# Second parity's keys and queries by seven block products, its values beside FFN chunks 0 and 1

## The chip, the cores and the metric

The kernel runs as one launch on one core of a Trainium2 chip. The metric is the device time of that launch in microseconds (us); smaller is better. A core has a matrix engine (PE in the profile, with PEld for its weight loads), two elementwise engines (DVE and ACT), a slower one that here only issues accumulating transfers (POOL), and SP, which issues most of the transfers. Each engine works through its own list of instructions, and instructions wait on semaphores for other engines and for transfers.

## What is computed

Input x has 2048 tokens of 512 channels. Two branches are mixed by a gate per token:

```python
g = sigmoid((x * gate_w).sum(-1, keepdims=True))
q, k, v = split(x @ wqkv)          # 32 heads of 16
# each token attends to itself and 7 earlier tokens at distance 2, 4, ... 14
a = softmax(q . k_window / 4) . v_window @ wo
b = (gelu(x @ w_gate) * (x @ w_up)) @ w_down     # 1792 hidden columns
out = g * a + (1 - g) * b
```

All of it is fp32.

## The kernel before, in words

**Tokens.** A token attends only to tokens of its own parity (the distance is even), so the program works through the even tokens and then through the odd ones: `par` 0 and 1. A parity has 8 tiles of 128 tokens (`jj`), in two blocks of four (`blk`). The 512 input channels are four chunks `kc` of 128.

**Products.** An fp32 operand is split into a high part (a copy to fp32r, "hi") and the rest ("lo", a subtraction); a product is three matmuls, hi.hi, lo.hi and hi.lo. So a tile of 128 tokens by 512 columns over two chunks is 6 matmuls, and a block product (four tiles) 24.

**Seven products.** Where a product is a 2 by 2 of blocks (two token blocks, two halves of the channels, two halves of the columns), `start()` for the keys and queries of the first parity and `gate_up()` for each FFN chunk form seven block products in place of eight: a11.b11, a12.b21, s1.t1, s2.t2, s3.t3, s4.b22 and a22.t4, where s1 to s4 are sums of blocks of x and t1 to t4 sums of blocks of the weights. The second parity's keys and queries are not formed so: `project(1, 0)` (L221) makes those of the first 16 heads (column block `cb` 0) tile by tile with 12 matmuls of 512 columns, and `project_one` (L251) those of the other 16 heads (`cb` 2), again 12 for each tile. `qkv_mm` (L183) issues them.

**Order of the program.** `start()` (from L842) loads x and the weights of the first parity, makes its keys and queries and prepares FFN chunk 0. `ffn(0)` runs 14 FFN chunks (`gate_up` and, two chunks behind, `down`); the first parity's values (`values`) run between its first products. Then comes what I call the turn: `project(1, 0)`, the split of more weights, `project(1, 1)` (the values), then `ffn(1)`, whose chunks 0 and 1 have the tiles of `project_one` between their products. In the last chunk (13) of `ffn(0)` the steps of `before()` and, after it, of `again` and `split_kq` prepare the turn: x of the second parity is split on DVE (copy and subtraction), and the weights of the first 16 heads, which `early()` loads in chunk 12, by ACT and DVE. The sums of x for the FFN are made by `sums_x()` within `project(1, 0)`.

**Attention.** It runs on DVE as a generator of small steps, pulled by credit (`pull`) as the matmuls are written: per unit of 8 heads (`par`, `u`) four pairs of score products (L290, L293), a softmax, and four pairs of weighted sums (L331 to L339). A unit's keys and queries go through HBM (`KS`, `QS`) and are loaded shifted (`load_kq`), the values likewise (`VS`, L274 and L275), and so are the outputs (`OS`, L346), which the output projection at the end reads (`finish`).

**What sets the order.** The scheduler of the language places instructions on their engines by its own estimate of time; `high_priority` puts attention behind the matmul chain, `paced` ties an instruction to the last matmul written, and the helper `Row` (`row`, `act`, `mms`) keeps the DVE, ACT and PE instructions written through it in the order written. Buffers are rings by tag: `raw` (2), `S` (8), `g0` and `g1` (2 each), `d` (4), `s` (3), `c` (4), `r` (2), PSUM banks `p` (4) and `acc0` to `acc3`. A tile of a ring waits until the tile that had its place has been read.

**Lines that the steps touch.** L107 loads x of the second parity into `raw`; L532 copies a running sum from SBUF to a PSUM bank before a `down`, L554 back; L549 scales the last `down` of parity 0 into an `s` tile and L550 sends it to the output by POOL; L452 and L453 (ACT, then a POOL transfer that accumulates) form the lo part of FFN weights, L457 the hi part; L464 and L470 store FFN weight sums and parts for the second parity; L590 and L606 are the two GELUs of a chunk, and L606's first after an exponential loads its table.

Of the kernel before, what the change touches and what calls it, by code (L numbers as in the profile page):

```python
# [16 lines left out]
P = 128  # L17
# [16 lines left out]
FILLERS = 2  # L34
BEHIND = 150
PACE = (0.9, 1.0, 1.12)
LOAD = 4.0
BT = 4
# [9 lines left out]
def tile_gated_mix(ctx: ExitStack, tc: tile.TileContext, xt, wqkv, wff, wo, out):  # L48
# [66 lines left out]
    def split_x(par, blk, kc, cols=((0, 512),), copy=None, eng=nc.vector):  # L115
        if blk and kc < 2:
            X[par, blk, kc] = tl("rt", F32R), tl("rt", F32R)
        hi, lo = X[par, blk, kc]
        raw = XR[kc % 2][:, (2 * blk + kc // 2) * 512:]
        for a, n in cols:  # L120
            c = slice(a, a + n)
            split(eng, hi[:, c], lo[:, c], raw[:, c], copy)

    def sums_x():

        for n in ("s1", "s2", "s4", "s3"):
            for kc in range(2):
                XOP[n, kc] = pair("S")
        for kc in range(2):
            a11, a12, a21, a22 = (XR[kc][:, i * 512:(i + 1) * 512] for i in range(4))  # L130
            nc.vector.tensor_tensor(a22, a21, a22, op=OP.add)
            nc.vector.tensor_tensor(a21, a11, a21, op=OP.subtract)
            nc.vector.tensor_tensor(a11, a22, a11, op=OP.subtract)
            nc.vector.tensor_tensor(a12, a12, a11, op=OP.subtract)
            for n, x in ("s1", a22), ("s2", a11), ("s4", a12), ("s3", a21):
                split(nc.vector, *XOP[n, kc], x)
                yield

    def rooms():

        def of(*tags):
            for tag, n in tags:
                t = tl(tag, F32R)
                w = 512 if n == 4 else WA
                yield from (t[:, i * w:(i + 1) * w] for i in range(n))
        cols = of(("g1", 4))
        for _ in range(2):
            yield next(cols), next(cols)
        for _ in range(2):
            yield pair("S")  # L150
        cols = of(("g0", 3), ("g1", 3), ("c", 1), ("c", 1))
        for _ in range(KC):
            yield next(cols), next(cols)
        for _ in range(KC):
            yield pair("d")

    def load_kq_weights(raw, kc):
        nc.sync.dma_start(raw[:, :512], wqkv[0, kc // 2, :, kc % 2 * 512:kc % 2 * 512 + 512])

    def held(o, i):  # L160
        return paced(nc.scalar.activation(o, i, AF.Copy))

    def load_cb(cb, kc, tag, room, late=False):
        hi, lo = WC[cb, kc] = next(room)
        raw = tl(tag)
        n = 512
        if cb == 1:
            nc.sync.dma_start(raw[:, :CU], wqkv[1, 2, :, kc * WQ:kc * WQ + CU])
            nc.sync.dma_start(raw[:, CU:CU + WQ], wqkv[0, 2, :, kc * WQ:(kc + 1) * WQ])
            n = CU + WQ  # L170
        else:

            queue = nc.scalar if cb == 0 and kc < 2 else nc.sync
            queue.dma_start(raw[:, :n], wqkv[cb // 2, kc // 2, :, kc % 2 * 512:kc % 2 * 512 + 512])
        return lambda: split(nc.vector, hi[:, :n], lo[:, :n], raw[:, :n], held if late else None)
# [4 lines left out]
    names = iter(["acc0", "acc1", "acc2", "acc3", *["p"] * 4])  # L180
# [27 lines left out]
    def take(ps, par, jj, hh, vals, tag=None):  # L208
        st = tl(tag or next(stages))[:, :512]
        n = CU if vals else 512  # L210
        nc.scalar.activation(st[:, :n], ps[:, :n], AF.Copy)
        two = st.rearrange("p (a c d) -> p a c d", a=2, c=2)
        dst = VS[par, hh] if vals else KS[par, hh]
        queue = nc.sync if (vals if par else not vals) or hh and not vals else nc.scalar
        queue.dma_start(rows(dst[:, W:], jj), two[:, 0])
        if not vals:
            queue.dma_start(rows(QS[par, hh], jj), two[:, 1])
        elif not hh:
            nc.scalar.activation(z[:, par, jj:jj + 1], ps[:, CU:CU + 1], AF.Copy)

    def project(par, cb, bg=iter(())):  # L221
        for jj in range(NP):
            if cb == 1:
                for hh in range(2):

                    ps = bank(f"acc{(2 * jj + hh) % BT}")
                    qkv_mm(ps, par, jj, 1, range(KC), (CU, 0)[hh], (WQ, CU)[hh])
                    take(ps, par, jj, hh, True)
            else:
                ps = bank(next(names))  # L230
                qkv_mm(ps, par, jj, 0, range(KC))
                take(ps, par, jj, 0, False)
            next(bg, None)
            pull((2.7, 2.2)[par])
        done.add((par, cb))
    def gates(par, ex):
        ordered(nc.scalar.activation(en, z[:, par], AF.Exp, scale=-1.0), ex)
# [4 lines left out]
    def values(jj):  # L242
        for hh in range(2):
            ps = bank(f"acc{(2 * jj + hh) % BT}")
            qkv_mm(ps, 0, jj, 1, range(KC), (CU, 0)[hh], (WQ, CU)[hh])
            take(ps, 0, jj, hh, True, tag=None if jj < 5 else "c")
        pull(2.7)
        if jj == NP - 1:
            done.add((0, 1))

    def project_one(par, jj):  # L251

        ps = bank(f"acc{jj % BT}")
        qkv_mm(ps, par, jj, 2, range(KC))
        take(ps, par, jj, 1, False, tag=None if jj < 5 else "c")
        pull(2.2)
        if jj == NP - 1:
            done.add((par, 2))

# [41 lines left out]
    def softmax(par, u):  # L301
# [7 lines left out]
        if not u:  # L309
# [4 lines left out]
        nc.vector.reciprocal(m, m)  # L314
        nc.vector.tensor_tensor(m, m, g[:, par, None, :].to_broadcast([P, UH, NP]), op=OP.mult)
# [51 lines left out]
    def attention():  # L367
# [8 lines left out]
        for i, un in enumerate(units):  # L376
            if scored == i:
# [5 lines left out]
                mixed = False  # L383
            yield from softmax(*un)

# [224 lines left out]
    SPLIT = []  # L610

    def again(blk, kc):

        split_x(1, blk, kc, copy=lambda *x: paced(nc.vector.tensor_copy(*x)))
# [9 lines left out]
    def split_kq():  # L624
        kc, raw = SPLIT.pop(0)
        hi, lo = WC[0, kc] = next(room)
        split(nc.vector, hi, lo, raw, held)

    def before():

        room_x(1)
        yield
        again(0, 0)
        yield
        again(0, 2)
        yield
        split_kq()
        SPLIT.append((3, tl("r")))
        load_kq_weights(SPLIT[-1][1], 3)
        yield  # L640
        split_kq()

    def ffn(par):
# [3 lines left out]
        for f in range(FC):  # L647
# [38 lines left out]
            else:  # L686
# [8 lines left out]
                if f + 2 == FC:  # L695
                    at(8, early)
# [474 lines left out]
```

## Time and profile before

| | |
|---|---|
| median of 3 runs | 605.52 us (605.47 to 606.92) |
| the profiled execution | 605.68 us, of which 603.9 us are the span of instructions |
| PE busy | 597.0 us, 99% of the span, 2802 matmuls |
| DVE busy | 525.1 us, 87% |
| ACT busy | 383.4 us, 63% |
| granted TensorE clock | 0.999 |
| HBM read, written | 67.18 MB, 36.77 MB |

The profile gives, for each engine, the time in which instructions ran. Matmuls are pipelined, so the length of one in the profile (390 ns for 512 columns) is not the distance between two; that is read from the starts of a run of them. The views used are: the page's totals, the list of waits (who waited for whom), the timeline of one engine (start, length, instruction, idle time before it and what ended it), busy time by stretch, and the transfers by line with their time from issue to landing.

### The profile page before, as it was taken

To read this page: it belongs to the slowest core of one execution; us is meant where nothing else is said; L and a number is where in the kernel's file an instruction comes from. 1 tells how busy PE (TensorE), PEld (TensorE's weight loads), DVE (VectorE), ACT (ScalarE), POOL (GpSimd) and SP (SyncE) were. 2 spreads that over 40 slices of the span, in tenths; PEclk is the share of its full clock that TensorE was granted. 3 is DMA by queue.
4 is the path that set the end of the run, shared out by engine and by line. 5 is a ranking of instruction groups with operands and counts; after the bars stand their busy time and mean duration, and the time that the engine had idled before them with its cause. 6 is when DMAs were issued, how large, how long until landed. Compare 5 with 4: busy or idle time off the path is not lost.

```text
span 603.9 us, 8190 instructions
## 1 busy us (share of the span) xinstructions
PE 597.0 (99%) x2802; PEld 497.9 (82%) x2802; DVE 525.1 (87%) x611; ACT 383.4 (63%) x650; POOL 79.0 (13%) x106
## 2 busy tenths in 40 slices
PE   9999999999999999999999999999999999999997
PEld 6889977788888888878899888888888888888885
DVE  5998869999898999898989978879899999998941
ACT  6845557787678767875553356565866676677531
POOL 0501001111111111102000001111111111101200
PEclk9999999999999999999999999999999999999999
DMA  7289886999889898967889968786887768837823
GB/s 282 84 257 243 244 268 175 277 240 255 238 246 259 222 271 213 263 197 205 261 253 292 299 191 242 169 249 179 209 221 202 210 174 228 245 90 204 115 63 139
DMA packets 84741, 131.03 MB, mean 217 GB/s; under 512 B 8030, under 2 KB 52317, under 8 KB 84700
## 3 DMA queue, kind: packets, MB, share of 16 engines
q1 hardware_dynamic: 63310, 94.01, 48.2%
q0 software_dynamic: 12096, 31.40, 27.6%
q10 hardware_dynamic: 9294, 5.11, 2.8%
q8 instruction: 22, 0.36, 0.3%
q14 instruction: 19, 0.16, 0.1%
HBM read 67.18 MB, written 36.77 MB: 172 GB/s over the span
## 4 chain that ended last, share of the span: by engine, by line
PE 87%; DMA 5%; DVE 3%; ACT 3%; issue 1%; SPq 1%; DVEq 0%; ACTq 0%
PE p L495 40%; PE p L538 12%; PE acc L538 12%; PE acc L189 9%; PE p L767 5%; PE p L834 3%; PE acc L834 3%; PE p L189 2%; PE acc L767 2%; DMA kq<-qs 1%; DMA raw<-wff 1%; DVE prod L290 1%; DMA ws<-g 1%; DMA raw<-xt 1%; DMA ks<-hl 0%
## 5 line engine op out<-in xcount | busy, mean ns | idle before, releaser
L495 PE MATMUL p<-S,g 128*128 128x512 f32 x672 | 166.5, 390 | 0.1
L495 PEld LDWEIGHTS p<-S,g 128*128 128x128 f32 x672 | 125.7, 188 | 26.6 <-ACT rt L554 0.5
L495 PE MATMUL p<-A,g 128*128 128x512 f32 x504 | 127.6, 390 | 0.0
L495 PEld LDWEIGHTS p<-A,g 128*128 128x128 f32 x504 | 94.3, 188 | 19.9 <-DVE c L505 0.3
L290 DVE TENSOR_TENSOR prod<-kq 128x2048 f32<-128x2048 f32 x32 | 73.0, 2282 | 10.1 <-DMA kq<-qs 5.1
L453 POOL DMA_DIRECT2D g<-raw x40 | 34.6, 866 | 334.8 <-ACT g L452 208.1
L331 DVE TENSOR_TENSOR prod<-v,lg 128x2048 f32<-128x2048 f32 x32 | 72.9, 2277 | 5.3 <-PE acc L538 2.5
L293 DVE TENSOR_REDUCE lg<-prod 128x128 f32<-128x2048 f32 x32 | 73.0, 2283 | 0.3
L538 PE MATMUL p<-d,hh 128*128 128x512 f32 x224 | 68.1, 390 | 1.0 <-ACT hh L511 0.5
L538 PE MATMUL acc<-d,hh 128*128 128x512 f32 x224 | 62.1, 391 | 0.5 <-DVE d L87 0.5
L538 PEld LDWEIGHTS p<-d,hh 128*128 128x128 f32 x224 | 41.8, 188 | 10.5 <-ACT hh L511 0.9
L538 PEld LDWEIGHTS acc<-d,hh 128*128 128x128 f32 x224 | 41.9, 188 | 10.2 <-DVE d L87 0.9
L457 ACT ACTIVATE g<-raw 128x1024 fp32r<-128x1024 f32 (+1 forms) x40 | 39.5, 990 | 13.2 <-PE p L495 13.2
L452 ACT ACTIVATE g<-raw 128x1024 fp32r<-128x1024 f32 (+1 forms) x40 | 39.4, 985 | 5.9 <-DVE raw L434 4.8
L505 DVE TENSOR_TENSOR c<-p,s 128x512 f32<-128x512 f32 x56 | 37.9, 681 | 5.6 <-PE p L495 5.6
L509 DVE TENSOR_TENSOR c<-c 128x512 f32<-128x512 f32 x56 | 38.2, 683 | 4.9 <-ACT c L606 4.8
L538 PE MATMUL p<-d,hl 128*128 128x512 f32 x112 | 42.3, 389 | 0.0
L500 ACT ACTIVATE s<-p 128x512 f32<-128x512 f32 x56 | 33.2, 592 | 13.6 <-PE p L495 11.8
L512 DVE TENSOR_TENSOR hl<-c,hh 128x512 fp32r<-128x512 f32 x56 | 38.2, 684 | 2.7 <-ACT hh L511 2.5
L511 ACT ACTIVATE hh<-c 128x512 fp32r<-128x512 f32 x56 | 35.1, 626 | 8.4 <-DVE c L509 7.7
L335 DVE TENSOR_TENSOR prod<-prod 128x1024 f32<-128x1024 f32 x32 | 39.0, 1220 | 0.4
L554 ACT ACTIVATE rt<-p 128x512 f32<-128x512 f32 x48 | 28.1, 593 | 16.2 <-PE p L538 15.9
(193 smaller groups left out, 915.7 us busy)
## 6 DMA issues: line engine op xcount, KB each, us to landing
g<-raw POOLq DMA_DIRECT2D x27, 512.0 KB, 6.5
raw<-wff SPq DMA_DIRECT2D x42, 256.0 KB, 3.2
ws<-g SPq DMA_DIRECT2D x14, 768.0 KB, 5.6
g<-ws SPq DMA_DIRECT2D x14, 768.0 KB, 6.1
r<-wff SPq DMA_DIRECT2D x28, 256.0 KB, 3.9
d<-r POOLq DMA_DIRECT2D x26, 256.0 KB, 6.6
g<-raw POOLq DMA_DIRECT2D x13, 384.0 KB, 6.3
v<-vs SPq DMA_DIRECT2D x8, 512.0 KB, 7.6
```

The costliest lines, as they stand in the source:

```text
L189: LAST[:] = [nc.tensor.matmul(ps[:, :cn], a[:, t], w[:, c0:c0 + cn], start=(kc == 0 and n == 0), stop=(kc == KC - 1 and n == 2))]
L290: paced(nc.vector.tensor_tensor(prod, spans(k, jj), q[:, jj:jj + 2, None, :].to_broadcast([P, 2, W, UC]), op=OP.mult))
L293: nc.vector.tensor_reduce(two_of(lg, jj), prod.rearrange("p j w (h d) -> p (j w) h d", d=DH), axis=AX.X, op=OP.add)
L331: paced(nc.vector.tensor_tensor(prod.rearrange("p j w (h d) -> p (j w) h d", d=DH), spans(v, jj).rearrange("p j w (h d) -> p j w h d", d=D ...
L335: nc.vector.tensor_tensor(prod[:, :, :4], prod[:, :, :4], prod[:, :, 4:], op=OP.add)
L452: nc.scalar.activation(lo, raw, AF.Copy, scale=-1.0)
L457: ins = nc.scalar.activation(hi, raw, AF.Copy)
L495: LAST[:] = [nc.tensor.matmul(ps, w_, a_, start=(start and kc == 0 and n == 0), stop=(kc == 1 and n == 2), skip_group_check=True)]
L509: nc.vector.tensor_tensor(ge, ge, up, op=OP.mult)
L512: nc.vector.tensor_tensor(hl_, ge, hh_.bitcast(F32), op=OP.subtract)
L538: ins = nc.tensor.matmul(pp, a[:, ts], w, start=(i == 0 and n == 0 and gr == 0), stop=(i == 1 and n == 2), skip_group_check=True)
L767: ins = nc.tensor.matmul(pa, a, b, start=(first and n == 0), stop=(last and n == 2), skip_group_check=True)
```

## The change

1. The first parity's weight sums t1 to t4, split into parts, are stored to HBM when they have been made (1 MB each, `store`), so that the second parity can load them (`load`).
2. `project`, `project_one`, `sums_x`, `again`, `split_kq`, `early`, `load_cb` and `rooms` go. In chunk 13 of `ffn(0)` and beside its last downs, `before()` and `ready()` load the raw blocks b11, b21 and b22 of the weights, split a11, a12, b11 and b21 (hi on ACT, lo on DVE) and make and split s1.
3. `kq_second()` makes the second parity's keys and queries by seven block products, in the order a11.b11, a12.b21, s2.t2, s3.t3, a22.t4 (after which the first 16 heads are complete), s1.t1, s4.b22. Attention steps are pulled after each tile (`ASK`).
4. The second parity's values move into chunks 0 and 1 of `ffn(1)`, in the place of `project_one`; the down weights of chunks 0 and 1 are split as in the first parity.
5. The first unit of the second parity does its softmax without the gate, then the scores of the second unit, and only then waits for the values (`gated`).

```diff
-    def early():
-        t = tl("g0")
-        for kc in range(3):
-            raw = t[:, kc * 512:(kc + 1) * 512]
-            load_kq_weights(raw, kc)
-            SPLIT.append((kc, raw))
...
     def before():
         room_x(1)
+        for k in range(2):
+            for i, (n, blk, kc) in enumerate((("a11", 0, 0), ("a12", 0, 2))):
+                OP_[n, k], SRC[n, k] = X[1, blk, kc + k], XR[k][:, i * 512:(i + 1) * 512]
+        load_raw("b11", slots("g1", 4), 0, 0)
         yield
-        again(0, 0)
-        yield
-        again(0, 2)
-        yield
-        split_kq()
-        SPLIT.append((3, tl("r")))
-        load_kq_weights(SPLIT[-1][1], 3)
-        yield
-        split_kq()
+        for step in (("a11", 0), (), (), ("a11", 1), ("a12", 0)):
+            if step:
+                hi(*step)
+                lo(*step)
+            yield
...
+    def load_raw(n, rooms_, hh, half):
+        raw = tl("S")
+        nc.sync.dma_start(raw, wqkv[hh, half, :, :1024])
+        name(n, pairs(rooms_), halves(raw))
+    def store(n, i, t, m):
+        nc.sync.dma_start(TS[n][i:i + m].rearrange("i p c -> p i c"), tiled(t, m))
+    def load(n, i, t, m):
+        nc.sync.dma_start(tiled(t, m), TS[n][i:i + m].rearrange("i p c -> p i c"))
...
+    def ready():
+        q = Q2["q"] = [[XR[k][:, i * 512:(i + 1) * 512] for i in range(4)] for k in range(2)]
+        load_raw("b21", slots("g0", 3, WA) + slots("c", 1), 0, 1)
+        load_pairs("t2")
+        yield
+        for steps in (("b11", 0),), (("b11", 1),), (("a12", 1), ("b21", 0)), (("b21", 1),):
+            for step in steps:
+                hi(*step)
+                lo(*step)
+            yield
+        load_raw("b22", [None] * 4, 1, 1)
...
+    def kq_second():
+        load("t4", 0, t, 4)
+        for i, tag in enumerate("sssc"):
+            t = tl(tag, F32R)
+            load("t3", i, t, 1)
+        U = [bank(f"acc{t}") for t in range(BT)]
+        block(U, "a11", "b11", True, ask=ASK)
+        V_ = [bank("p") for _ in range(BT)]
+        for t in range(BT):
+            out_of(V_[t], U[t])
+        block(V_, "a12", "b21", False, ask=ASK)
...
+        block(U, "s2", "t2", False, ask=ASK)
+        block(U, "s3", "t3", False, ask=ASK)
+        block(U, "a22", "t4", False, ask=ASK)
+        done.add((1, 0))
+        block(Z_, "s1", "t1", True, ask=ASK)
+        for t in range(BT):
+            join(1, BT + t, Z_[t], u3[t])
+        block(Z_, "s4", "b22", False, ask=ASK)
+        for t in range(BT):
+            join(1, t, Z_[t], u2[t])
+        done.add((1, 2))
...
-    room = rooms()
     keep(0)
     ffn(0)
-    for kc in range(KC):
-        load_cb(1, kc, "c", room)()
-    project(1, 0, sums_x())
-    for kc in range(KC):
-        load_cb(2, kc, "r", room, True)()
-    fetch_d(0)
-    for f in range(2):
-        fetch_sums(f)
-    project(1, 1, chain(*(operands(1, 0, i) for i in range(2))))
+    kq_second()
     ffn(1)
```

More of the change, by code (lines that the diff above doesn't have):

```diff
@@ L34 @@
 FILLERS = 2
+ASK = 1.0
 BEHIND = 150
@@ L113, in room_x @@
             X[par, blk, kc] = pair("A")
[L115 to L136, printed above, removed]
-                yield
@@ L707, in ffn @@
             oT = {}
+        else:
+            Q2["turn"] = ready()
         for b in range(2):
@@ L712, in ffn @@
                     oT[0, b] = channels(par, 0, b)
[L713 to L716 removed]
+                if not par:
+                    next(Q2["turn"], None)
         if par:
@@ new lines, in hi, with lo, both, sub @@
+    def hi(n, k):
+        act.activation(OP_[n, k][0], SRC[n, k], AF.Copy)
+    def lo(n, k):
+        h, l = OP_[n, k]
+        row.tensor_tensor(l, SRC[n, k], h.bitcast(F32), op=OP.subtract)
+    def both(f, *ns):
+        for n in ns:
+            for k in range(2):
+                f(n, k)
+    def sub(o, a, b):
+        row.tensor_tensor(o, a, b, op=OP.subtract)
+    def mm(ps, t, a, w, first=False, last=False):
+        LAST[:] = [mms.matmul(ps, a[:, t * P:(t + 1) * P], w, start=first, stop=last, skip_group_check=True)]
@@ L999, in start @@
         shift(nc.sync, 0, BT - 1)
+        for k in range(2):
+            store("t1", 2 * k, d_[k], 2)
         Z_ = [bank("p") for _ in range(BT)]
@@ L1025, in start @@
         out_of(p5[3], Z_[3])
+        for k in range(2):
+            store("t2", 2 * k, d_[2 + k], 2)
         block(U, "s2", "t2", False)
```

300 lines of the change are left out of this document (164 added, 136 removed).

## The prediction

> **What bounds the kernel now.** I read the page's totals first, then the list of waits of PE, then PE's timeline where the removed matmuls stand.
>
> ```profile
> span 603.9 us, 8190 instructions
> PE 597.0 (99%) x2802; PEld 497.9 (82%) x2802; DVE 525.1 (87%) x611; ACT 383.4 (63%) x650; POOL 79.0 (13%) x106
> PE p L538 <- ACT p L532: 0.5, 1, 0.5
> PE acc L538 <- DVE d L87: 0.5, 1, 0.5
> 334.65 5.60 PE L189 MATMUL acc<-d,A 128*128 128x512 f32 x24
> 340.09 1.30 PE L495 MATMUL p<-A,g 128*128 128x512 f32 x5
> 280.23 3.34 PE L189 MATMUL acc<-g,A 128*128 128x512 f32 x14
> ```
>
> The second line is the argument: PE is busy 99% of the span, DVE 87%. The third and fourth are two of PE's few waits, half a microsecond each, one on ACT's copy of a running sum, one on DVE's lo part of a down weight. So the time is the number of matmuls times their distance, as long as nothing comes late to PE; and the change can be slower in one way only, by new waits of PE. The distance is read from the fifth and sixth: 24 matmuls from 334.65 to 340.09 are 5.44 us, 0.2267 us each. The turn, where most of the change lies, begins at 280.23.
>
> **The change part by part.** The profiled execution took 605.68 us, 1.8 more than its span; the median is 605.52, so the sum is made on 605.68 and stands for both.
>
> *A. Matmuls.* Two column blocks of 8 tiles with 12 matmuls are 192; seven block products with 24 are 168. The values' narrow matmuls are the same number at another place. 24 x 0.2267 = **-5.44 us**, all of it on the bound engine. I found nothing on PE to set against it: the order of the built program (it has no times in it) shows no other matmul added.
>
> *B. Stores at the start.* t1 to t4 are 4 MB on SP's queue, some 29 transfers more over the program, the loads at the turn included. I read busy time by stretch (PE, PEld, DVE, ACT, POOL, then granted clock, DMA share, GB/s) and DVE's and PE's timelines after it.
>
> ```profile
> 25.00:30.00 5.00, 5.00 (x24) 4.14 (x23) 4.69 (x8) 4.51 (x9) 0.79 (x2) 1.00 0.32 107
> 30.00:35.00 5.00, 5.00 (x24) 4.14 (x23) 5.00 (x9) 2.91 (x6) 0.00 (x0) 1.00 0.77 209
> 35.00:40.00 5.00, 5.00 (x24) 4.14 (x23) 4.76 (x8) 2.20 (x4) 0.00 (x0) 1.00 0.96 291
> 40.00:45.00 5.00, 5.00 (x25) 3.90 (x23) 4.47 (x9) 1.91 (x5) 0.00 (x0) 1.00 0.88 263
> 45.00:50.00 5.00, 5.00 (x33) 4.57 (x33) 4.93 (x8) 3.63 (x11) 0.00 (x0) 1.00 0.67 208
> 55.00:60.00 5.00, 5.00 (x44) 5.00 (x43) 4.86 (x3) 1.32 (x4) 0.00 (x0) 1.00 1.08 225
> 62.37 0.69 DVE L434 TENSOR_TENSOR raw<-raw 128x512 f32<-128x512 f32 x1 [1.66 <-DMA raw<-wff]
> 82.12 2.29 DVE L290 TENSOR_TENSOR prod<-kq 128x2048 f32<-128x2048 f32 x1 [5.08 <-DMA kq<-qs]
> 87.99 0.50 PE L538 MATMUL acc<-d,hh 128*128 128x512 f32 x1 [0.48 <-DVE d L87]
> ```
>
> t1 and t2 are stored while DMA is a third busy (first line). t3 and t4, 2 MB, follow in 30 to 50 us; at the 291 GB/s of the third line they take 7 us, and the stretches have 1.2 + 0.2 + 0.6 + 1.6 = 3.6 us free. So 3.4 us of transfers are pushed on, into stretches that are full (1.08). DVE already waits there for `raw` (1.66 us) and 20 us on for `kq` (5.08 us); that `kq` buffer is loaded when DVE's scores before it are done, so lateness in the first wait comes back in the second. Six microseconds behind stands the lo part that PE waits for at 87.99, with no slack (it waits 0.48 now). Ends: 0.3 us if the push is swallowed by free DMA time at 65 to 70 us, 5 if all of it and a DVE instruction of 0.69 arrive. I take **+2.5**, near the full push less one microsecond.
>
> *C. Chunk 13, ACT.* Now a hi copy of x's second half stands in ACT's list ahead of the GELU's table load and of the copy (L532) that PE's next down needs; three copies of x and four of raw weights b11 and b21 stand ahead of the copy after that. Rows: PE's two downs, ACT in between, and SP's transfers.
>
> ```profile
> 263.80 0.61 PE L538 MATMUL p<-d,hh 128*128 128x512 f32 x2
> 267.88 0.61 PE L538 MATMUL p<-d,hh 128*128 128x512 f32 x2
> 257.07 0.62 ACT L481 ACTIVATE d<-r 128x512 fp32r<-128x512 f32 x1
> 257.71 1.28 ACT L606 ACT_TABLE_LOAD   x1
> 259.63 0.60 ACT L532 ACTIVATE p<-rt 128x512 f32<-128x512 f32 x1
> 265.01 0.59 ACT L532 ACTIVATE p<-rt 128x512 f32<-128x512 f32 x1
> 249.73 1.28 SPq L158 DMA_DIRECT2D g<-wqkv  x3
> 259.79 1.21 SPq L107 DMA_DIRECT2D raw<-xt  x2
> SPq L107 <- DMA ws<-raw: 8.2, 1, 8.2
> raw<-xt SPq DMA_DIRECT2D x2, 512.0 KB, 5.5
> 250.48 0.86 POOL L453 DMA_DIRECT2D g<-raw  x1 [3.40 <-ACT g L452]
> g<-raw POOLq DMA_DIRECT2D x1, 512.0 KB, 9.0
> ```
>
> Before, x is asked for at 259.79, after 8.2 us of waiting for a store of `raw`, behind three loads of weights (249.73) and an accumulating transfer (250.48) that took 9.0 us. The three loads, 768 KB, go: at the 9.0 us of the last row for 512 KB being the crowded pace, I put x's issue at 257, bounds 253 and 259.8. It takes 5.5, so x is there at 262 (bounds 258.2 and 265.3). ACT stands still until then: copy, table load, GELU and the first copy for PE are 0.6 + 1.28 + 0.6 + 0.6, ready at about 264.7, against 263.80: PE is late by 0.9. Eleven instructions at 0.52 to 0.6 each (259.63 to 265.01 held seven, with gaps) lead to the second copy, ready at 264.7 + 11 x 0.52 + 0.6 = 271.0 against 267.88. **+3.0**, bounds: 0.6 at the early end (where b21, asked for at about 261 when its `S` buffers are free and 5.5 us under way, takes x's place as the last to come), 6 at the late end.
>
> The Trainium skill, page "DMA: Bandwidth & Descriptors", section "Measured (HBM→SBUF, 128 partitions, SWDGE, issued from GpSimd)", has 1 MB in 6.15 us; an estimate from that page for 512 KB would be 3.1 to 3.5, and the sum below would be about 2 us lower by it. This trace has 5.5 for 512 KB, and it decides.
>
> *D. The turn.* Block a12.b21 adds into PSUM banks that ACT first fills with copies of a11.b11; two of these copies stand in ACT's list behind the seventh and eighth scaling of the last outputs (L549), and t3 is loaded into the same `s` ring of three. Rows of ACT and POOL, and the output's transfer.
>
> ```profile
> 287.92 1.33 ACT L549 ACTIVATE s<-p,gc 128x512 f32<-128x512 f32 x2 [4.97 <-DMA out<-s]
> 282.05 1.74 POOL L550 DMA_DIRECT2D out<-s  x3 [1.60 <-ACT s L549]
> out<-s POOLq DMA_DIRECT2D x8, 256.0 KB, 4.4
> ```
>
> Now the seventh scaling stands until 287.92 for an output to land. Block a11.b11 begins where L189 began, 280.23, and lasts 5.44, to 285.67; the third and fourth copies would be there at 288 to 289.3, when PE has done the two tiles before (2.7 us, to 288.4): about 1 us of wait, and 0.7 more for two copies in one line. For t3, with 512 KB of t2 and 1 MB of t1 and t4 on the same queue, I add a microsecond. Ends: 0.5 (transfers are 3 us faster with less else under way) and 6 (one more transfer of 4.4 behind another). I take **+2.5**.
>
> *E. FFN of the second parity.* Attention now comes later: the first unit's outputs, keys and queries pass SP's queue behind the loads of the turn.
>
> ```profile
> 316.29 0.69 DVE L87 TENSOR_TENSOR d<-r,d 128x512 fp32r<-128x512 f32 x1 [2.42 <-ACT d L161]
> 316.90 0.68 DVE L337 TENSOR_TENSOR prod<-prod 128x512 f32<-128x512 f32 x1
> 330.31 2.25 DVE L290 TENSOR_TENSOR prod<-kq 128x2048 f32<-128x2048 f32 x1
> 361.00:577.00 216.00, 216.00 (x955) 178.85 (x954) 196.73 (x213) 142.16 (x231) 30.41 (x36) 1.00 0.77 195
> 576.81 0.71 DVE L344 STREAM_TRANSPOSE tb<-o 128x512 f32<-128x512 f32 x1
> 584.85 0.69 DVE L87 TENSOR_TENSOR hl<-raw,hh 128x512 fp32r<-128x512 f32 x1 [2.71 <-ACT hh L86]
> 594.41 0.61 PE L767 MATMUL p<-S,hh 128*128 128x512 f32 x2
> ```
>
> The first scores of the second parity began at 330.31. Block a22.t4, which completes those heads, ends at 280.23 + 5 x 5.44 = 307.4 plus the waits of C and D, about 313; the copies, stores, loads and the FFN's preparations (eight 0.69 us subtractions more on DVE) put the scores at some 344 to 347 by my count of what stands ahead of them on SP and DVE. That is 14 to 17 us late. DVE has 216 - 196.73 = 19.3 us idle up to the last transpose at 576.81, and the last split, over at 585.5, is used at 594.41: 8.9 us to spare. So the end holds; but in between DVE runs with less reserve before each FFN step, and PE's wait can show at a few of them. Ends 0 and 4; I take **+1**, near the low end, because DVE's FFN steps stand ahead of attention in the order.
>
> That DVE and ACT keep to their list is what C and D rest on, and this trace shows it: at 316.29 a subtraction waited 2.42 us for ACT, and the weighted sum behind it, whose input was there, ran only at 316.90. The Trainium skill, page "PSUM — Partial Sum Buffer", section "Engine vs sequencer instructions", says so too ("ScalarE/VectorE/GpSimdE queues are strict FIFO"), which speaks against this change.
>
> **Sum.** 605.68 - 5.44 + 2.5 + 3.0 + 2.5 + 1.0 = **609.2 us**.
>
> **Rivals.** *The saving is just eaten* (B to E together 4 to 7 us): about 605.6. For it: each wait is worked out with half-known issue times, and a late PE gives the next supplier time, so the four terms do not add in full. *Faster:* the transfers come before ACT reaches them. It decides whether x is asked for by 253 and the second copy is ready by 267.88. Then C is 0.6, B one subtraction of 0.69, D 0.5 and E nothing: 605.68 - 5.44 + 1.8 = 602.0, or 600.3 with no wait at all. For it: 99% busy PE shows that nearly all transfers are in time now, and the turn had 0.5 us of waits with much the same traffic. Against it: the rows of 4.97, 5.08 and 8.2 us say that several are already late and only PE does not see it. *DVE sets the end, slower:* if the 19.3 us idle cannot be used (they are waits for ACT and PE), 17 us of lateness pass through whole, less 8.9 to spare: 605.68 + 8.1 = 613.8; it decides when the last transpose falls later than about 586. Against it: those idle times lie before FFN steps, where a late attention step fits. *The change doesn't do what it says:* the built program has 24 matmuls fewer, so no.
>
> **How the numbers follow.** About 0.3% (1.8 us) is what a measurement of this kernel can tell from no change: faster is below 603.7, slower above 607.3. Forecast, 609.2 (607.3 to 613): 0.45. DVE-bound end, 613.8: 0.13. Saving just eaten, 605.6: 0.19. Faster, 602: 0.23. So slower 0.58, same 0.19, faster 0.23. The range leaves out the very end of each side: 600.8 (a little above no wait at all) to 615.5 (the DVE end with part of the turn's waits).
>
> **What the changed profile would show.** A: 24 matmuls fewer, same distance. B: DVE's waits for `raw` at 62 us and `kq` at 82 longer, PE's at 88 two microseconds or more. C: ACT idle some 3 us before the copy of x's second part, and PE's waits on the two copies of sums at 264 and 268. D: PE waits before the second and fourth block product at the turn. E: the second parity's scores after 340 us, the last transpose still before 586. Wrong would be the forecast if x is asked for at 253 to 255, if PE's total wait stays below 4 us, or if the waits lie at a place not named here.

## The result, and the profile after

The changed kernel takes 624.53 us (median of four executions, 623.63 to 625.53) against 606.03 for the kernel before: 1.030 times as long, with a 95% interval of 1.028 to 1.033. The forecast was 609.2, with a range of 600.8 to 615.5; the time lies outside it. The profiled execution took 625.53, 19.85 more than the 605.68 of before. In the experiments, one execution of the run without stores (its profiled one) ran at a granted clock of 0.753 throughout and is not used.

First the page's totals:

```profile
span 623.8 us, 8180 instructions
PE 603.1 (97%) x2778; PEld 498.3 (80%) x2778; DVE 525.0 (84%) x611; ACT 390.6 (63%) x660; POOL 77.3 (12%) x104
```

The span and mean granted clock of the core:

```profile
core 0: 623.8 us, clock 0.984
```

And PE's list of waits (us in total, times, longest):

```profile
PE p L465 <- ACT p L459: 4.3, 2, 4.0
PE acc L465 <- DVE d L88: 3.3, 1, 3.3
PE p L422 <- ACT s L427: 2.4, 1, 2.4
PE acc L738 <- DMA s<-wt: 2.1, 1, 2.1
PE p L738 <- ACT p L738: 0.9, 1, 0.9
```

The 24 matmuls are gone (2802 to 2778), and yet PE is busy for 6 us more. Its waits add up to 17.1 us (2.9 before). The clock has the rest: 0.984, not the 0.999 of before. Over 623.8 us that is 10.2 us lost. Where it was lost is seen in the busy time by 2 us (the columns as in the prediction; the granted clock is the third number from the end):

```profile
86.00:88.00 2.00, 1.23 (x5) 1.05 (x6) 1.97 (x2) 2.00 (x5) 0.00 (x0) 1.00 1.14 207
88.00:90.00 2.00, 2.00 (x6) 1.52 (x5) 2.00 (x2) 1.92 (x3) 0.00 (x0) 0.55 0.96 200
276.00:278.00 2.00, 0.26 (x1) 0.26 (x2) 2.00 (x4) 2.00 (x5) 0.00 (x0) 0.50 0.13 43
278.00:280.00 2.00, 2.00 (x5) 1.56 (x6) 2.00 (x4) 0.21 (x1) 0.00 (x0) 0.50 0.00 0
314.00:316.00 2.00, 2.00 (x6) 1.51 (x6) 0.00 (x0) 0.56 (x1) 0.00 (x0) 0.50 0.75 313
384.00:386.00 2.00, 2.00 (x6) 1.60 (x5) 2.00 (x2) 0.00 (x0) 0.00 (x0) 0.50 1.01 342
```

There are four stretches at half clock, each behind or over the end of one of the four long waits. The trace gives their lengths: 3.41, 6.83, 3.41 and 6.83 us, so one or two times 3.41, 20.5 us together. The view counts the matmuls that touch a stretch of 2 us: six here, eleven at full clock.

Of the 20.5 us at half clock PE was busy for 17.4, so 8.7 us were lost by the clock; for the rest PE stood, and that time is in the waits already. The sum of the profiled execution: 605.68 - 5.44 + 14.2 of waits + 8.7 of clock = 623.1, and 2.4 us over for the slower first matmuls behind a wait and small pieces. This is the account of one execution. The other three had a mean clock of 0.989 to 0.992, so they lost some 5 to 7 us by the clock where this one lost 10.2, and still took 623.63 to 624.65: what the clock doesn't take there, other things do.

Now the four places, in order of time. **Start**, first DMA's share (the last number but one) in the stretch before:

```profile
40.00:50.00 10.00, 10.00 (x56) 8.47 (x55) 9.41 (x16) 6.15 (x14) 0.00 (x0) 1.00 0.95 309
```

Then ACT, DVE and PE:

```profile
54.10 0.85 ACT L379 ACTIVATE g<-raw 128x768 fp32r<-128x768 f32 x1 [5.45 <-DMA kq<-kq]
67.58 0.69 DVE L361 TENSOR_TENSOR raw<-raw 128x512 f32<-128x512 f32 x1 [2.50 <-DMA raw<-wff]
85.64 0.60 ACT L533 ACTIVATE c<-p 128x512 f32<-128x512 f32 x1 [1.33 <-DMA vs<-c]
86.77 1.75 PE L422 MATMUL p<-S,g 128*128 128x512 f32 x6 [2.37 <-ACT s L427]
```

DMA is full (0.95; 0.88 and 0.67 in the two halves of this stretch before). ACT stands 5.45 us in its own list for the shift of `kq`, and at 85 us it stands again, for a store of values that has not landed. **Chunk 13** (SP, ACT, PE):

```profile
260.70 1.21 SPq L108 DMA_DIRECT2D raw<-xt  x2
266.10 0.63 ACT L738 ACTIVATE A<-raw 128x512 fp32r<-128x512 f32 x1 [3.34 <-DMA raw<-xt]
273.52 1.15 ACT L738 ACTIVATE g<-S 128x512 fp32r<-128x512 f32 x2 [2.20 <-DMA S<-wqkv]
277.74 1.22 PE L465 MATMUL p<-d,hh 128*128 128x512 f32 x2 [4.02 <-ACT p L459]
```

ACT waits 3.34 us for x and 2.20 for b11, and the copied sum behind them is 4 us late. The transfers of 512 KB (size and us to landing, 250 to 290 us):

```profile
S<-wqkv SPq DMA_DIRECT2D x3, 512.0 KB, 8.3
raw<-xt SPq DMA_DIRECT2D x2, 512.0 KB, 6.5
```

The raw weights took 8.3 us from issue to landing (the median of three), x 6.5, against 5.5 for x before. **The turn** and **the stretch behind it** (ACT and PE; then DVE and PE):

```profile
301.45 0.69 ACT L476 ACTIVATE s<-p,gc 128x512 f32<-128x512 f32 x1 [2.32 <-DMA out<-s]
302.81 1.43 PE L738 MATMUL p<-g,A 128*128 128x512 f32 x5 [0.95 <-ACT p L738]
312.82 0.73 PE L738 MATMUL acc<-s,S 128*128 128x512 f32 x2 [2.05 <-DMA s<-wt]
354.29 0.69 DVE L432 TENSOR_TENSOR c<-p,s 128x512 f32<-128x512 f32 x1 [10.14 <-PE p L422]
364.54 2.29 DVE L203 TENSOR_TENSOR prod<-kq 128x2048 f32<-128x2048 f32 x1 [8.76 <-DMA kq<-qs]
382.25 1.28 DVE L88 TENSOR_TENSOR d<-r,d 128x512 fp32r<-128x512 f32 x2
382.99 0.80 PE L465 MATMUL acc<-d,hh 128*128 128x512 f32 x1 [3.35 <-DVE d L88]
```

DVE, which before had 19.3 us without work between 361 and 577 us, now has nothing to do for nearly 20 us (10.14 + 8.76) because the keys and queries of the second parity are not loaded (SP issues their load at 356.51 us); then it is packed, and the lo part of a down weight, whose hi part was there at 378, is made behind the scores.

### The profile page after: what moved, and what is told of

It is laid out like the page before. It is cut to its first block, busy times and chain, and to the rows that moved or that the text cites. A ratio compares the mean times of both kernels' runs of the same rounds, so it can differ in the third digit from the quotient of the medians.

```text
span 623.8 us, 8180 instructions
## 1 busy us (share of the span) xinstructions
PE 603.1 (97%) x2778; PEld 498.3 (80%) x2778; DVE 525.0 (84%) x611; ACT 390.6 (63%) x660; POOL 77.3 (12%) x104
## 4 chain that ended last, share of the span: by engine, by line
PE 72%; issue 10%; DMA 8%; DVE 4%; ACT 4%; SPq 1%; POOL 1%; ACTq 0%; POOLq 0%; DVEq 0%
PE p L422 33%; PE acc L465 10%; PE p L465 9%; PE acc L738 5%; PE p L671 5%; PE p L738 4%; PE acc L130 3%; DMA vs<-c 2%; PE acc L671 2%; DMA raw<-wff 2%; DMA ws<-g 1%; DVE prod L203 1%; DMA vs<-hh 1%; DMA s<-wt 1%; DMA raw<-xt 1%
## 5 line engine op out<-in xcount | busy, mean ns | idle before, releaser
L422 PE MATMUL p<-S,g 128*128 128x512 f32 x672 | 168.8, 392 | 3.5 <-ACT s L427 2.4
L465 PE MATMUL p<-d,hh 128*128 128x512 f32 x224 | 70.5, 400 | 4.9 <-ACT p L459 4.3
L384 ACT ACTIVATE g<-raw 128x1024 fp32r<-128x1024 f32 (+1 forms) x40 | 39.5, 989 | 19.4 <-PE p L422 19.3
L481 ACT ACTIVATE rt<-p 128x512 f32<-128x512 f32 x48 | 28.1, 594 | 17.3 <-PE p L465 17.1
```

The source lines that it names most:

```text
L384: ins = nc.scalar.activation(hi, raw, AF.Copy)
L422: LAST[:] = [nc.tensor.matmul(ps, w_, a_, start=(start and kc == 0 and n == 0), stop=(kc == 1 and n == 2), skip_group_check=True)]
L465: ins = nc.tensor.matmul(pp, a[:, ts], w, start=(i == 0 and n == 0 and gr == 0), stop=(i == 1 and n == 2), skip_group_check=True)
```

## Experiments

My theory after the result: four causes, each a wait in a list kept in order, and behind each a price of the clock. The times, each with the kernel before on the same chip:

| run | us (median) | before | ratio, 95% interval |
|---|---|---|---|
| changed kernel | 624.5 | 606.0 | 1.028 to 1.033 |
| e1_no_stores | 621.7 (three executions) | 606.4 | 1.019 to 1.029 |
| e8_before_stores | 610.5 | 606.1 | 1.005 to 1.010 |
| e2_hi_behind | 622.3 | 606.4 | 1.025 to 1.031 |
| e7_hi_last | 618.8 | 606.1 | 1.016 to 1.024 |
| e5_t3_early | 623.2 | 606.1 | 1.022 to 1.030 |
| e3_kq_early | 620.6 | 606.4 | 1.022 to 1.030 |
| e12_values | 626.8 | 606.2 | 1.029 to 1.037 |
| e12_both | 618.2 | 606.2 | 1.015 to 1.022 |
| e4_busy | 623.4 | 606.4 | 1.025 to 1.032 |
| e9_three | 615.4 | 606.4 | 1.012 to 1.022 |
| e9_three_ask | 622.0 | 606.4 | 1.022 to 1.030 |
| e10_raw | 618.7 | 606.4 | 1.020 to 1.023 |
| e11_outs | 613.8 | 605.9 | 1.010 to 1.018 |
| e11_all | 609.7 | 605.9 | 1.005 to 1.008 |
| e11_act | 616.1 | 605.9 | 1.015 to 1.021 |

**What an idle time of PE costs.**

> Not the reference's computation: PE alone, bursts of 100 matmuls of 512 columns (22.7 us) with an idle time of PE between them that a chain of ACT copies makes, 20 of them from about 1 to 7 us. Theory: up to some length (between 0.95 and 2.05 us by the changed kernel's waits) the granted clock stays full behind the idle time; above it the clock is at half for 3.41 us, and from some 3.3 us on for 6.83 us, so that an idle time costs itself and 1.7 or 3.4 us more. Rival: the half clock is none of the idle time's doing: no stretch of it, or stretches that don't follow the idle times.

The loop, abridged:

```python
for i in range(BURST):
    matmul(ps, a[:, i % 4 * P:(i % 4 + 1) * P], w if not i else a[:, 512:], ...)
activation(c[0], ps[:, :256], AF.Copy)
for i in range(n):
    activation(c[(i + 1) % 2], c[i % 2], AF.Copy)
activation(w[:, :64], c[n % 2][:, :64], AF.Copy)
```

PE's rows with the idle time ahead:

```profile
284.18 0.50 PE L77 MATMUL ps<-w,a 128*128 128x512 f32 x1 [2.10 <-ACT w L82]
81.50 0.80 PE L77 MATMUL ps<-w,a 128*128 128x512 f32 x1 [2.61 <-ACT w L82]
109.38 0.80 PE L77 MATMUL ps<-w,a 128*128 128x512 f32 x1 [3.51 <-ACT w L82]
200.22 0.80 PE L77 MATMUL ps<-w,a 128*128 128x512 f32 x1 [6.19 <-ACT w L82]
```

The 15 us that follow each of these four (the second number in brackets of a row is PEld's count, the first PE's matmuls):

```profile
284.18:299.18 15.00, 15.00 (x66) 12.40 (x67) 0.00 (x0) 0.00 (x0) 0.00 (x0) 1.00 0.00 0
81.50:96.50 15.00, 15.00 (x60) 12.33 (x61) 0.00 (x0) 0.00 (x0) 0.00 (x0) 0.90 0.01 1
109.38:124.38 15.00, 15.00 (x54) 12.15 (x55) 0.00 (x0) 0.00 (x0) 0.00 (x0) 0.81 0.00 0
200.22:215.22 15.00, 15.00 (x58) 12.28 (x59) 0.00 (x0) 0.00 (x0) 0.00 (x0) 0.88 0.01 1
```

The half clock is the idle time's doing. Idle times of 0.76, 1.27, 1.72 and 2.10 us left the clock full (66 matmuls in 15 us); each of the sixteen from 2.61 on had a stretch at half clock of 3.41, 6.83 or 10.24 us, and 6 to 13 matmuls (1.4 to 2.9 us) fewer in the 15 us behind it. But the length does not set the stretch, as I had expected: 3.51 us had 6.83 and 4.40 us had 3.41, and after 6.19 us the price was 8 matmuls only, since part of the stretch had passed while PE stood. In the changed kernel a wait of 2.05 us had its stretch, and one of 2.37 us had it there and had none in the next run below.

What decides is where the idle time falls. Within each trace all half-clock stretches begin on one grid of 3.413 us: in this run at 81.09, 108.39, 139.11 and 166.42 us, which are 8, 9 and 8 steps apart. Cut into these steps, the 17 traces of this case (all but that of the run without stores) follow one rule. From full clock, all 43 steps in which PE stood idle for 57% or more (1.96 us) were followed by half clock, and none of those with 55% or less was; once at half clock, PE stayed there behind the 20 steps with 17% or more of idle time, and had full clock again behind the 43 with 15% or less. Two steps each of the changed kernel and of e7_hi_last, which is treated below (the second number is PE's busy time):

```profile
84.79:88.21 3.42, 1.44 (x6) 1.22 (x7) 2.72 (x2) 2.58 (x5) 0.67 (x1) 1.00 0.97 196
88.21:91.62 3.41, 3.41 (x9) 2.67 (x9) 3.41 (x4) 2.34 (x4) 0.00 (x0) 0.50 0.96 235
372.03:375.44 3.41, 1.84 (x9) 1.18 (x7) 3.41 (x4) 1.13 (x3) 0.00 (x0) 1.00 1.06 312
375.44:378.86 3.42, 1.65 (x7) 1.39 (x8) 3.42 (x6) 1.42 (x2) 0.00 (x0) 1.00 0.70 159
```

In the first pair most of the wait of 2.37 us falls into one step, 58% of which is idle, and the next is at half clock. In the second a wait of 3.34 us is cut into 46% and 52%, and the clock stays full. The Trainium skill, page "TensorE: Matmul & The Clock Gate", section "What's actually happening", tells of a gate that halves PE's clock after an idle window of 3.413 us, which runs freely and does not begin with the work. The steps of 3.41 us and their fixed grid agree; but a window need not be idle as a whole, 58% of one was enough here.

**Does PE busy instead of idle keep the clock?**

> The changed kernel with dummy matmuls (zeros added to an open sum, 256 columns) in PE's list ahead of three of the matmuls that wait: 36 before the second copied sum of chunk 13, 18 in the fourth block product, 30 before the lo part of the down weight, about as long as the waits. No cause of a wait is taken away. Theory: the lower clock of 0.984 comes from PE standing idle; with PE busy through those waits the half-clock stretches behind them go (only the first, at 87 us, stays), the mean clock is 0.995 or more, and the time falls by up to 8 us, to 616 to 619. Rival: the clock falls for another reason (the kind of matmul, the load of the chip): 0.984 and 624.5 or more.

```diff
+        if not par and gr == NG - 2 and b and t == 3:
+            busy(ACC[3], 36)
...
+                if par and gr == b == t == i == n == 0:
+                    busy(pp, 30)
```

The core's span and clock in this run:

```profile
core 0: 618.7 us, clock 1.000
```

And its list of PE's waits:

```profile
PE p L422 <- DVE c L432: 2.9, 3, 1.4
PE p L422 <- ACT s L427: 2.4, 1, 2.4
PE p L752 <- ACT p L752: 2.0, 2, 1.6
```

(`busy` issues so many 256-column matmuls of zeros; the block product's 18 are not shown.) Half right. The stretches behind the three waits are gone, and in this execution the first one too, though its wait of 2.37 us still stands (the grid cuts it into 49% and 20%). But the time fell by less than forecast: 620.5 in the profiled execution, 623.4 in the median. At full clock PE came sooner to the next late sum, and waited there (2.9 us for DVE's sums, 2.0 in the turn). Some of the gain went to the extra matmuls themselves: the copied sum of chunk 13 was there at about 275.8 us, and they held PE until 276.66. So the clock's 8.7 us are not simply to be had, and the run does not say exactly how much of them is.

**The stores at the start.**

> The changed kernel without the eight stores of t1 to t4 at the start; at the turn, parts of FFN weights of the same size are loaded in their place, so the second parity's keys and queries are not those of the reference. Theory: the stores push the transfers of 30 to 60 us back, and through ACT (which stands for a landing at 52 us) make the 2.37 us wait of PE at 86.8 us and the half clock behind it; without them this wait is below 0.6 us, the clock stays full there, and the time falls by some 4 us, to about 620.5. Rival: the values' new place or the order of SP's list makes that wait, not the stores; then it stays and the time is within 1 us of 624.5.

```diff
     def store(n, i, t, m):
-        nc.sync.dma_start(TS[n][i:i + m].rearrange("i p c -> p i c"), tiled(t, m))
+        pass
```

> The kernel before, with nothing added but the stores of t1 to t4 at the start (nothing reads them). Theory: the stores alone make PE wait some 2.4 us near 83 us, with 3.4 us at half clock behind it: 609.5 to 611 against 606. Rival: the stores fit beside what is there and the wait came from the order of the list in the changed kernel: 605.5 to 607.

```diff
+        for k in range(2):
+            store("t1", 2 * k, d_[k], 2)
...
+        store("t4", 0, t4_, 4)
```

The kernel before with the stores alone has the changed kernel's wait, and one stretch of 3.41 us at half clock:

```profile
87.11 2.31 PE L495 MATMUL p<-S,g 128*128 128x512 f32 x6 [2.21 <-ACT s L500]
```

610.5 against 606.1: the stores cost 4.4 us. The changed kernel without them took 617.1 to 622.9 us, which fits and is too wide to say more. The length of the wait varies: in the nine other traces with the same start it is 1.49 to 3.34 us.

**Chunk 13.**

> The changed kernel with the hi copies of x's second part and of b11 and b21 put behind the copies of running sums in ACT's list (chunk 13). Theory: PE's waits of 0.30 and 4.02 us at 269 and 277 us come from these hi copies, which wait for x and b11; with them behind, both waits go, the clock stays full, and the time falls by 6 to 7.7 us, to some 617 to 618.5, unless the later hi copies make the first block product wait (at most 2 us of it back). Rival: the transfers are late whatever stands first, and the wait moves as a whole to the first block product: 624.5.

> As the run with the hi copies behind, but b11's and b21's also stand behind the third copied sum of the last downs. Theory: what was left of PE's wait in chunk 13 (3.43 us at 276.7 us) was ACT standing for b11 (3.69 us) ahead of the next copied sum; now no copied sum stands behind a load, the wait is below 1 us, and the time falls to 617 to 620. Rival: b11 and b21 come too late for any order; then the first or second block product waits 3 us and the time stays at 622 or more.

```diff
     def hi(n, k):
-        act.activation(OP_[n, k][0], SRC[n, k], AF.Copy)
+        ins = act.activation(OP_[n, k][0], SRC[n, k], AF.Copy)
+        if HOLD:
+            ordered(ins, HOLD[-1])
```

`HOLD` keeps the last copied sum behind which they stand. With x's copies behind, the copied sum at 268 us was in time and PE waited 3.43 us for the next one, which stood behind b11 (ACT's wait for it 3.69 us): the rival's picture, but one copy on, and 622.3 us in place of the 617 to 618.5 that I expected. With b11 and b21 behind as well, no wait over 0.65 us is left in the chunk and the clock stays full there:

```profile
280.67 2.12 PE L467 MATMUL acc<-d,hh 128*128 128x512 f32 x8 [0.64 <-ACT hh L438]
```

The time falls by 5.7 us, to 618.8: it was ACT's order, not the landing.

**The turn.**

> The changed kernel with t3's four pieces loaded into the rt buffers, which are free between the last copied sums and a21, and not into the ring of the last outputs. Theory: the wait of 2.05 us in the fourth block product (312.8 us) is for buffers that the outputs still hold; it goes, and with it the 3.4 us at half clock behind it: some 620.7, or up to 2 us more if the other waits take part of it back. Rival: the transfers of this stretch are limited by bandwidth, so that t3 in time makes another load late; PE waits as long elsewhere, 624.5.

```diff
-        for i, tag in enumerate("sssc"):
-            t = tl(tag, F32R)
+        for i in range(4):
+            t = tl("rt", F32R)
             load("t3", i, t, 1)
```

The wait for t3 goes, and the time falls by 1.3 us only, which is within the scatter of the two kernels: PE waits 2.34 us for DVE at 369 us (0.56 in the changed kernel) and 3.36 at 382. The rival had the time right but named bandwidth as the cause; the trace has DVE. What is won ahead of the stretch behind the turn is given back there, as long as DVE is late in it (the next runs).

**Behind the turn.**

> The changed kernel with one move: the load of the second parity's first keys and queries is written as soon as they are stored, not when attention has come to them. Theory: DVE's idle time at 344 to 364 us comes from this load standing in SP's list behind stores that wait for DVE and ACT, and it makes DVE late with the lo part of a down weight (PE's wait of 3.35 us at 383 us, and the half clock behind it); with the load early DVE starts the scores before 350 us, that wait falls below 1 us, and the time falls by 5 to 7 us, to 617.5 to 619.5. Rival: the wait is the down weights' split on DVE itself, with no preparation by POOL: it stays, and the time is 623.5 to 625.

> The changed kernel with one edit: the second parity's values are stored by POOL's queue, not SP's. Theory: the load of the second parity's first keys and queries and the values' buffers no longer stand in SP's list behind one another; DVE's idle time of 8.8 us before the scores (364 us) shrinks by half or more, PE's wait of 3.35 us at 383 us falls below 2 us, and the time falls by 2 to 6 us, to 618.5 to 622.5. Rival: the place of that load behind attention in the list decides alone; the wait stays and the time is within 1 us of 624.5.

> As e12_values, and the load of those keys and queries written behind the loads of the first FFN sums. Theory: both hold DVE back, and with both gone the whole price of the stretch from 340 to 400 us (7.3 us: 3.9 of waits, 3.4 of half clock) goes: 616.5 to 618.5. Rival: the transfers of the stretch are limited by bandwidth; PE waits 3 us or more elsewhere in it, 620 to 624.

```diff
+        load_kq(1, 0)
...
-        (nc.sync if par else nc.scalar).dma_start(rows(VS[par, hh][:, W:], jj), two)
+        (nc.gpsimd if par else nc.scalar).dma_start(rows(VS[par, hh][:, W:], jj), two)
```

Rows of e3_kq_early (ACT and PE), and below of e12_values (DVE):

```profile
347.66 1.06 ACT L380 ACTIVATE g<-raw 128x1024 fp32r<-128x1024 f32 x1 [8.62 <-DMA raw<-wff]
349.11 2.54 PE L130 MATMUL acc<-d,A 128*128 128x258 f32 x11 [3.91 <-ACT z L155]
```

```profile
359.71 2.29 DVE L203 TENSOR_TENSOR prod<-kq 128x2048 f32<-128x2048 f32 x1 [20.36 <-DMA kq<-qs]
```

Loading the keys and queries early starts the scores at 346 us and ends the wait at 382; the time falls by 3.9 us, to 620.6. In the profiled execution, at 625.3 the slowest of its four, an FFN load is now late, ACT stands 8.62 us and PE 3.91. Taking the values off SP's list alone gains nothing (626.8; the profiled execution, 621.9, is the fastest): the scores begin at 359.71, some 5 us earlier, but DVE still has no work for 20.36 us, as against 10.14 + 8.76, and now the sum that PE needs stands behind the scores in DVE's list, so that PE waits 3.94 us for it. Both together: PE's list of waits is empty from 325 us to the end, and the time is 618.2. That is 6.3 us, of a price of 6.7 in this stretch (3.9 of waits, 2.8 of clock). The load's place in SP's list is needed for that. How much the number of transfers in the list adds is not shown here, because e3 has the load at another place than e12_both; e11_outs and e11_all below, with the same place, show it.

**All of them.**

> Three repairs together: the hi copies behind the copied sums (as e7), t3 in the rt buffers (as e5), and the load of the first keys and queries written behind the loads of the first FFN chunks' sums, not behind attention. Theory: the waits of chunk 13, of the fourth block product and of the down weight's lo part go together, because none stands for another; left are the stores' 4.4 us at the start, some 2 us in the turn and the matmuls' saving of 5.4: 607 to 610. Rival: the stretch from 330 to 370 us is limited by transfers, so that keys and queries in time make FFN loads or stores late, and PE waits 3 us or more there again: 612 to 616.

> The same three repairs, with attention asked for 1.5 us of steps after each tile of the seven products in place of 1.0. Theory: the last weighted sums of the first parity end some 8 us earlier, DVE starts the second parity's scores as soon as they are loaded, and has more reserve at 380 us: 0 to 3 us below the run with 1.0. Rival: attention's steps stand in DVE's list ahead of the splits that the block products need; PE waits in the turn: 2 us above it or more.

> The three repairs, and t3 and t4 stored as plain sums (0.5 MB each in place of 1 MB) and split again at the turn by four hi copies on ACT and four subtractions on DVE: 1 MB less is stored at the start and 1 MB less loaded at the turn. Theory: with half of the late stores gone, half or more of the 4.4 us at the start goes, and the turn's transfers are earlier, against 2.6 us of DVE at the turn: 2 to 4 us below the three repairs alone. Rival: the wait at the start is that of the load that must follow a store into the same buffer; then it stays or grows, and the time is equal or above.

> The three repairs with plain sums of t3 and t4 (as e10), and the last five of the first parity's outputs scaled into hh and hl tiles, not into the ring of three s tiles. Theory: PE's wait of 4.73 us for the copies of a11.b11 in the turn (292 us, and 6.8 us at half clock behind it, 8.1 us in all) is ACT standing for an output to land ahead of those copies; it goes, and the time falls from 618.7 to 611 to 614. Rival: DVE and the transfers behind the turn set the time; the 8 us are given back before 400 us and it is 616 or more.

> As e11_outs, and the second parity's values are stored by POOL's queue, not SP's. Theory: ACT's wait of 8.52 us near 355 us for stores of values (they stand in SP's list behind keys, queries and outputs, one every 0.45 us) is what makes DVE stand for the gate and PE wait 2.1 us at 368; it goes too: 606 to 610. Rival: the landing, not the issue, is late (bandwidth): within 1 us of e11_outs.

> As e11_all, with the values stored by ACT's own queue, as in the first parity. Theory: the same relief of SP, but each store costs ACT some 0.4 us in its list: 606 to 611, within 2 us of e11_all. Rival: ACT's issues stand for earlier stores and hold up its copies: 614 or more.

```diff
+        store_raw("t3", b12)
...
-            st = tl("s")
+            st = tl("s" if jj < 3 else ("hh", "hl")[jj % 2])[:, :512]
...
-ASK = 1.0
+ASK = 1.5
```

(The first line is in e10 and e11, the second edit in e11, the last in e9_three_ask; the values' queue is edited as above.)

Three repairs give 615.4, 9.2 us below the changed kernel, and none of the 3.35 us for the down weight is left; but I had expected 607 to 610. PE's 2.96 us in the turn, with a stretch at half clock behind them, are the copies that stand behind the outputs; in the changed kernel they cost 0.95. Attention asked for faster is worse (622.0), as its rival said, but not mainly for its reason: of PE's waits for DVE only 1.01 us lie in the turn, 1.99 at 376 us and 2.49 at 547. Plain sums of t3 and t4 take away PE's wait of 2.4 us at 87 (in all four traces that have them), with only half of the two stores gone; they are also issued earlier, before the split, so it is not shown which of the two does it. But the turn then had 4.73 us for the copies of a11.b11 and the time rose to 618.7. Outputs in other buffers halve that wait (2.32 left): 613.8. The reason for ACT's longest wait behind the turn, here its row in e10_raw,

```profile
363.84 0.39 ACT L151 ACTIVATE c<-acc 128x256 f32<-128x256 f32 x1 [8.52 <-DMA vs<-c]
```

was mostly SP's list: e11_outs with the values on POOL's queue took 609.7, and ACT's wait fell from 6.72 to 3.59 us. On ACT's own queue it took 616.1, with a wait of PE for ACT of 5.84 us. The Trainium skill, page "DMA: Bandwidth & Descriptors", section "Issuing engines are not separate DMA queues", holds that more issuing engines save only the usually small time of issuing; here, where the list is kept in order and stands for other engines, they saved 4.2 us. The best of these versions, at full clock in all but one of its executions (0.999 there), still stands 0.6% above the kernel before. Its longest wait of PE, behind the row of ACT that leads to it:

```profile
287.88 0.69 ACT L479 ACTIVATE hh<-p,gc 128x512 f32<-128x512 f32 x1 [5.61 <-PE p L468]
290.84 1.43 PE L744 MATMUL p<-g,A 128*128 128x512 f32 x5 [2.32 <-ACT p L744]
```

No landing is behind this one: ACT waits for PE's last downs, and then four scalings of outputs (to 290.17) stand ahead of the copies that PE needs. This wait and eight of 0.4 to 1.1 us make up 7.3 us (2.9 before), and PE's busy time is only 2.2 us shorter than before (594.8 against 597.0), not 5.4. So the 5.44 us saved are eaten by many small losses. Whether an order exists that has none of them stays open.

## Why the prediction was wrong

**The bound and A: right.** PE sets the time, and 5.44 us of matmuls went.

**The step that failed is the sum's unit.** The prediction said that the change can be slower "by new waits of PE" only, and counted each at its length. A wait of 2 us and more was followed by 3.41 or 6.83 us at half clock: 8.7 us that stand in none of the terms. The trace of before could not show them, its longest wait being 1.1 us. The waits too were larger: 14.2 us against 9.0. With 2.4 us of small pieces, these are the 16.3 us by which the profiled execution lies above 609.2. The parts are not independent: with PE kept busy through three of the waits (e4) the median fell by only 1.2 us.

**B, 2.5: the size of the wait was met (2.37), partly by luck, since it is 1.49 to 3.34 in other traces; the way was not.** I let the push go through DVE's `raw` and `kq` to the lo part at 88 us. DVE's wait for `raw` did grow (2.50 against 1.66), but that for `kq` shrank (3.21 against 5.08). ACT was first: it issues the shift of `kq` and the values' stores itself and stood for their landings. With the clock the stores cost 4.4 (e8), inside the range of 0.3 to 5.

**C, 3.0: the mechanism as forecast, the size too low.** x was issued at 260.70, some 256 when the 4.3 to 5.1 us by which PE was late are taken off, against my 257. The waits were 4.3 us. Part of that is my addition: 257 + 5.5 + 3.1 is 265.6, not 264.7, and the term would have been 4.0. And I had b11 in time with 5.5 us of transfer; it took 8.3 and cost ACT another 2.20. The estimate of about 3.3 us by the Trainium skill's page ("DMA: Bandwidth & Descriptors", section "Measured (HBM→SBUF, 128 partitions, SWDGE, issued from GpSimd)") would have led further off. The clock's share (2.5) made it 6.8. e7 shows the cause.

**D, 2.5: right in the total of the waits**, 3.0, and less so in the parts: 0.95 for the copies behind the outputs, where I had 1.7, and 2.05 for t3, where I had 1. The clock added 1.7. But that it counts by itself was wrong: e5 took one of them away and got 1.3 us.

**E, 1.0: mis-sized.** The waits were 3.9 and the price 6.7. I put the scores at 344 to 347 us; they began at 364.54, because the load of keys and queries stood in SP's list behind stores that waited for DVE and ACT. And I took the low end because DVE's FFN steps stand ahead of attention; the lo part of the down weight stood behind it. e12_both takes nearly the whole away.

**The rivals.** The one that has DVE set the end did not happen: PE's losses were made before 400 us, and no wait above 0.5 us follows. Its sign misled, though: the last transpose fell at 599.88, not before 586, because PE itself was some 20 us late by then. What came was none of the rivals: all four terms together, with the clock on top. My argument that the four terms do not add in full was true only of edits that undo one of them.

## What to carry to other kernels

Where PE is busy 99% of the span, price a new wait by more than its length. Here one that left PE idle for 57% of a 3.41 us step cost 1.4 to 2.9 us more in a run of PE alone; keeping PE busy through three such waits won only 1.2 us in the changed kernel (e4), where other engines were late behind them. Take a microsecond won in front of another late engine for nothing. In every list that is kept in order (ACT's copies, SP's transfers), look for what waits for a transfer and stands ahead of something that PE needs; here another order of the same work was worth 5.7 us on ACT, and 16 transfers moved from one list to another 4 us.

## What the runs showed of the hardware

The half clock came in steps of 3.41 us on a fixed grid. A step with PE idle for 57% or more set it off and one with 55% or less did not, so a wait of 2.01 us (e12_values) had its stretch and one of 3.34 us (e7) had none. The stores at the start cost 4.4 us for 4 MB; with t3 and t4 at half size and issued earlier, 1 MB fewer, PE's wait of 2.4 us there was gone.
